# Normalised attention rows copied by a transfer and transposed as float32r with a lag of four slots; token rows transposed as float32r

## The chip, the cores and the metric

The kernel runs on one core of one Trainium2 chip. The metric is the device time of one execution in microseconds (us), lower is better; where several executions are timed, their median counts. All profile rows come from one profiled execution of the same program.

## The reference

Gated causal attention over 8 batches of 8 heads, 576 tokens, head dimension 64, followed by a normalised two-layer feed-forward network on the 4608 tokens of width 512. Everything is float32.

```python
scores = scale * (q @ k.T) + cum[:, None] - cum[None, :]      # cum: cumulative log of the gate f
attn = softmax(where(causal, scores, -1e9))
x = concat_heads(attn @ v)                                     # (8, 576, 512)
xn = (x - mean(x)) / sqrt(var(x) + 1e-6) * g_ln
out = x + relu(xn @ w_ch1) @ w_ch2                             # 512 -> 2048 -> 512
```

## The kernel before

**Slots.** The order of the work is written out by hand. The attention is cut into 256 *slots*, four for each of the 64 heads: slot t (1 to 4) takes 128 rows of queries, and t = 1 also the first 64 rows (called t = 0). `QT` gives each block's first row, its number of rows and the width `w` of keys that it can see: 64, 192, 320, 448, 576. For each slot a string of letters in `ORDERS` says in which order the pieces are recorded on all engines; from slot 70 on this is `"WwAthQFlMSPNgreamLRB"`. The pieces that matter here:

- `Q` multiplies the queries of the slot with the keys (TensorE, tile `s`, lines 368 to 373). `S` (line 396, VectorE) adds the mask into tile `p` and takes the row maximum, `e` (line 407, ScalarE) exponentiates, and `B` (`normalise`, lines 412 to 414) takes the reciprocal on VectorE and multiplies the rows by it on GpSimd. `p` has three buffers; the 64 rows of t = 0 have their own tile of 64 columns (`corner`).
- `t` (`transpose_unit`) transposes the normalised rows of the slot `LAG` = 2 slots back, in pieces of 64 or 128 columns: 3, 3, 4 and 5 transposes for t = 1, 2, 3, 4, so 15 in each head. The rows are the operand that is loaded into the array and the identity is streamed. Both are float32. The result (tiles `tr`, `tr_4b`) goes to `ph` as float32r by ScalarE (`h`, line 476), and from head 12 on the rounding error goes to `pl` by VectorE (`l`, line 481).
- `A` multiplies with the values one slot after t = 2 and t = 4 were transposed (tile `o`, line 511), `F` and `a` bring the sum to `xs`, which is stored to DRAM.
- `P` prepares the next heads: `raw` (keys and queries, 576 KB) is loaded in slot t = 4 for the head after the next and cast to `hi` by ScalarE (line 339) in the next slot; `prep_v` and the load of the next values `vr` stand in slot t = 3.

**Feed-forward.** In each slot from number 35 on, if its operands are planned to be there, `M` does one of 16 steps of the first layer for a *chunk* of 256 tokens (12 matmuls, tile `h`, lines 588 to 590), `r` and `m` split the result into a float32r pair `hh` on ScalarE (line 596) and VectorE (line 601), and `N` does the second layer for the step of the slot before (6 matmuls, tile `acc`, lines 610 to 612). The halves `w2s` of the second layer's weights come from DRAM, three steps ahead (line 703). A chunk's operand `x` is loaded from the stored attention result (`xr`, line 621); `moe.limit` says how many chunks the attention has finished. Near a chunk's end `rows_load` brings its tokens once more (`xw`) and `chunk_rows` transposes them back to rows, eight float32 transposes for each chunk (tile `xp`), for the residual and the statistics. After the last slot the remaining steps run by themselves.

**Queues.** Every transfer is issued by SyncE (SP), in the order in which it is recorded; a transfer that waits holds all those behind it. PSUM has six banks for all of `s`, `tr`, `o`, `h` and `xp`, taken in turn.

The helper through which all transposes go:

```python
    def tr(out_, in_):
        m = in_.shape[0]
        nc.tensor.transpose(out_, in_, ident[:m, :m])
```

Of the kernel before, what the change touches and what calls it, by code (L numbers as in the profile page):

```python
# [8 lines left out]
F32 = mybir.dt.float32  # L9
F32R = mybir.dt.float32r  # L10
# [5 lines left out]
B, H, S, D = 8, 8, 576, 64  # L16
DM, DFF = H * D, 4 * H * D
P = 128
# [10 lines left out]
W2_LOW = 3  # L29
W2_WAIT = 2  # L30
ALL = 2 * NCHUNK * FT + W2_WAIT
LAG = 2
FIRST_MOE = 35
WARM = 36

# [16 lines left out]
ORDERS = [  # L52
    (0, "WwbQsSthAeMrgFmlLNPaRf"),
    (37, "WwbQSstAMhPelgLNFrfmBRa"),
    (70, "WwAthQFlMSPNgreamLRB"),
]


# [1 line left out]
def attn_moe(ctx: ExitStack, tc: tile.TileContext, qk, v, f, g, w1, w2, out):  # L60
# [245 lines left out]
    def load(n):  # L306
        h = Head()
        h.n, h.plain, h.full = n, n < NPLAIN, n < NFULL
        h.normal = {}
        if h.plain:  # L310
            h.kl = work.tile([66, S], F32, tag="kl", bufs=2, name=f"kl{n}")
            if len(xfs) < 2:
                xfs.append(new_xq(f"xf{n}", F32))
            h.xq = xfs[n % 2]
            nc.sync.dma_start(out=h.xq[0:64, :], in_=qk[n][0:64, 0, :])
            nc.sync.dma_start(out=h.kl[0:64, :], in_=qk[n][0:64, 1, :])
            if n > 0:
                nc.sync.dma_start(out=h.kl[64:66, :], in_=cumd[n])
            return h
        h.raw = late.tile([P, 2, S], F32, tag="raw", bufs=2, name=f"raw{n}")  # L320
        nc.sync.dma_start(out=h.raw, in_=qk[n])
        return h
# [95 lines left out]
    def normalise(h, t):  # L418
        h.normal[t] = True
        if t == 1:  # L420
            softmax_b(h, 0)
        softmax_b(h, t)

    def tr(out_, in_):
        m = in_.shape[0]
        nc.tensor.transpose(out_, in_, ident[:m, :m])  # L426

# [1 line left out]

    def transpose_unit(h, t):
        n = f"{h.n}"
        pt = h.p[t][0]
        work_ = []
        if t <= 2:
            if t == 1:
                h.ph1 = work.tile([P, 704], F32 if h.full else F32R, tag="ph1", bufs=1, name=f"ph1_{n}")
                h.pl1 = None if h.full else late.tile([P, 384], F32R, tag="pl1", bufs=1, name=f"pl1_{n}")
            ph = h.ph1  # L440
            pl = ph if h.full else h.pl1
            tp = bank(f"tr{n}_{t}")
            if t == 1:
                tr(tp[0:64, 0:128], h.p[0][0])
                tr(tp[0:64, 64:192], pt[:, 0:64])
                tr(tp[:, 192:320], pt[:, 64:192])
                work_.append((tp[0:64, 0:192], ph[0:64, 0:192], ph[64:128, 0:192]))
                work_.append((tp[:, 192:320], ph[:, 320:448], pl[:, 0:128]))
            else:
                tr(tp[0:64, 0:128], pt[:, 0:64])  # L450
                tr(tp[:, 128:256], pt[:, 64:192])
                tr(tp[:, 256:384], pt[:, 192:320])
                work_.append((tp[0:64, 0:128], ph[0:64, 192:320], ph[64:128, 192:320]))
                work_.append((tp[:, 128:384], ph[:, 448:704], pl[:, 128:384]))
        else:
            if t == 3:
                h.ph2 = work.tile([P, 9 * P], F32 if h.full else F32R, tag="ph2", bufs=1, name=f"ph2_{n}")
                h.pl2 = None if h.full else late.tile([P, 7 * P], F32R, tag="pl2", bufs=1, name=f"pl2_{n}")
            c = 0 if t == 3 else P
            ph = h.ph2[:, : 8 * P].rearrange("p (k c) -> p k c", k=4)[:, :, c : c + P]  # L460
            pl = None if h.full else h.pl2[:, : 6 * P].rearrange("p (k c) -> p k c", k=3)[:, :, c : c + P]
            tp = bank(f"tr{n}_{t}").rearrange("p (k c) -> p k c", k=4)
            tr(tp[0:64, 0, :], pt[:, 0:64])
            for k in range(1, 4):
                tr(tp[:, k, :], pt[:, 64 + P * (k - 1) : 64 + P * k])
            work_.append((tp[0:64, 0, :], ph[0:64, 0, :], ph[64:128, 0, :]))
            work_.append((tp[:, 1:4, :], ph[:, 1:4, :], pl))
            if t == 4:
                tp = bank(f"tr{n}_4b")[:, :P]
                tr(tp, pt[:, 64 + 3 * P : 64 + 4 * P])  # L470
                work_.append((tp, h.ph2[:, 8 * P :], None if h.full else h.pl2[:, 6 * P :]))
        h.parts = work_
# [156 lines left out]
    def chunk_rows(c, i):  # L629

        tp = bank(f"xp{c.n}_{i}")
        for k in range(KT):
            tr(tp[:, P * k : P * k + P], c.xw[:, k, :])
        xt = m2(f"xt{c.n}_{i}", F32)
        nc.scalar.copy(out=xt, in_=tp)
        if i == 0:
            c.sv = work.tile([P, 2, 2], F32, tag="sv", bufs=2, name=f"sv{c.n}")
            c.rs = work.tile([P, 4], F32, tag="rs", bufs=2, name=f"rs{c.n}")
        bs = work.tile([P, 6], F32, tag="bs", bufs=2, name=f"bs{c.n}_{i}")
        nc.vector.bn_stats(bs, xt)  # L640
        nc.vector.bn_aggr(c.sv[:, i, :], bs)
        c.xt.append(xt)
# [110 lines left out]

    slots = [(n, t) for n in range(B * H) for t in (1, 2, 3, 4)]
    nu = len(slots)
    slots += [None] * (LAG + 1)
    hd = {}

    def start_head(n):
# [10 lines left out]
    for u, slot in enumerate(slots):  # L770

        def before(k):
            return slots[u - k] if u >= k else None

        if slot is not None:
            n, t = slot
            h = hd[n]
        av = None
        if before(LAG + 1) is not None and before(LAG + 1)[1] in (2, 4):
            av = hd[before(LAG + 1)[0]]  # L780
        moe.fetch_low(ALL if wp.done() else wp.ready())
        want = moe.can(wp.ready()) and u >= FIRST_MOE

        def piece(c):
            tu = before(LAG)
            if c == "t" and tu is not None:
                transpose_unit(hd[tu[0]], tu[1])
            elif c == "h" and tu is not None:
                transposed_hi(hd[tu[0]], tu[1])
            elif c == "l" and tu is not None:  # L790
                transposed_lo(hd[tu[0]])
            elif c == "Q" and slot is not None:
                if t == 1:
                    qk_mm(h, 0)
                qk_mm(h, t)
            elif c == "A" and av is not None:
                av_unit(av, before(LAG + 1)[1])
            elif c == "S" and slot is not None:
                if t == 1:
                    softmax_a(h, 0)  # L800
                softmax_a(h, t)
            elif c == "e" and slot is not None:
                if t == 1:
                    softmax_e(h, 0)
                softmax_e(h, t)
            elif c in FILL:
                wp.fill(FILL[c])
            elif c == "s":
                wp.sums()
            elif c == "F" and av is not None:  # L810
                finish(av)
            elif c == "a" and av is not None:
                finish_add(av)
            elif c == "r" and want:
                moe.first_high()
            elif c == "R":
                moe.limit = min(NCHUNK, max(0, u - LAG - 1) // (4 * H) * S // C)
                moe.rest()
            elif c == "L":
                run_later(RSTD)  # L820
            elif c == "M" and want:
                moe.first()
            elif c == "B" and slot is not None:
                normalise(h, t)
            elif c == "b" and before(1) is not None:
                b_n, b_t = before(1)
                if not hd[b_n].normal.get(b_t):
                    normalise(hd[b_n], b_t)
            elif c == "m" and want:
                moe.first_low()  # L830
            elif c == "W":
                due = 1 + min(u, W_CHANGE) / W_SLOTS + max(0, u - W_CHANGE) * W_TICKS
                while not wp.done() and wp.tick_no <= due:
                    wp.tick()
            elif c == "N":
                moe.second()
            elif c == "P":
                prep()

        def prep():  # L840

            if slot is not None:
                if t == 1 and n + 1 < NPLAIN:
                    start_head(n + 1)
                if NPLAIN <= n + 1 < B * H:
                    if t == 1:
                        prep_a(hd[n + 1])
                    if t == 2:
                        prep_b(hd[n + 1])
                    if t == 3:  # L850
                        prep_c(hd[n + 1])
                if t == 4 and NPLAIN <= n + 2 < B * H:
                    start_head(n + 2)
                if not h.full and t == LAG + 1:
                    prep_v(h)
                if t == LAG + 1 and n + 1 < B * H:
                    load_v(hd[n + 1])

        for c in [o for first, o in ORDERS if first <= u][-1]:
            piece(c)  # L860
# [48 lines left out]
```

## Time and profile before

| | before |
|---|---|
| median of three runs | 1228.67 us (1228.44 to 1228.71) |
| profiled execution, its own time | 1229.45 us |
| span of the profiled instructions | 1227.4 us |
| TensorE matmuls (PE) busy | 1205.5 us, 98% of the span |
| weight loads (PEld), beside the matmuls | 1075.7 us, 88% |
| VectorE (DVE) / ScalarE (ACT) / GpSimd (POOL) | 62% / 53% / 35% |
| DMA queue q1 | 49.9% of 16 engines, 189.15 MB |
| mean granted TensorE clock | 0.994 |

A matmul's row in the trace has a start and a modelled end, and successive matmuls overlap, so the durations of a group may add up to more than the time it holds TensorE. What a matmul costs in a full stream is the distance from its start to the next start. In a row that joins several instructions ("x4") the second column runs from the first start to the last end.

### The profile page before, as it was taken

Reading aid. Unit: us, or ns where it says so; the run is one execution under the profiler, and the core shown is the slowest. Engines: PE = TensorE matmul, PEld = TensorE weight load, DVE = VectorE, ACT = ScalarE, POOL = GpSimd, SP = SyncE. Lnnn points to the kernel's source line nnn. Section 1 sums busy time; section 2 is a strip of 40 time slices with the busy share of each in tenths; the row PEclk is TensorE's granted clock in tenths of the full one; section 3 lists DMA queues with packets and bytes.
Section 4 is the critical chain, followed back from the end, with each engine's and each line's share of the span. In section 5 each row is a group of like instructions: output and inputs, shape, how many; then the busy total and the mean of one; then the engine's idle time right before and its main releaser. Section 6 shows DMA issues by size and latency. Waiting matters only on the chain.

```text
span 1227.4 us, 25515 instructions
## 1 busy us (share of the span) xinstructions
PE 1205.5 (98%) x8140; PEld 1075.7 (88%) x8140; DVE 762.5 (62%) x2884; ACT 646.3 (53%) x1920; POOL 425.9 (35%) x533
## 2 busy tenths in 40 slices
PE   7998999899999999999999999999999999999998
PEld 5665889889999999999999999999999999999997
DVE  5787647576767676677767676767676764233232
ACT  5888655455655555556555555556555653112111
POOL 3568534333333444343334343334334330000000
PEclk8999999999999999999999999999999999999999
DMA  6888554354545454455454445445454453443532
GB/s 175 249 244 270 175 163 152 104 162 147 164 139 160 143 153 150 155 173 168 151 168 141 145 148 168 156 140 166 140 156 146 153 154 100 143 125 117 148 109 95
DMA packets 138358, 190.78 MB, mean 155 GB/s; under 512 B 31216, under 2 KB 80624, under 8 KB 138224
## 3 DMA queue, kind: packets, MB, share of 16 engines
q1 hardware_dynamic: 138224, 189.15, 49.9%
q8 instruction: 65, 1.06, 0.3%
q14 instruction: 69, 0.57, 0.2%
HBM read 157.46 MB, written 23.36 MB: 147 GB/s over the span
## 4 chain that ended last, share of the span: by engine, by line
PE 90%; DMA 3%; DVE 3%; ACT 2%; issue 1%; SPq 0%; POOL 0%; DVEq 0%; ACTq 0%; POOLq 0%
PE h L588 11%; PE h L589 11%; PE h L590 11%; PE acc L610 10%; PE acc L611 10%; PE acc L612 10%; PE tr L426 7%; PE o L511 6%; PE s L372 3%; PE s L373 3%; PE o L489 3%; DMA raw<-in_qk_dram 2%; PE s L370 2%; PE xp L426 1%; PE pc L190 1%
## 5 line engine op out<-in xcount | busy, mean ns | idle before, releaser
L414 POOL TENSOR_SCALAR p<-p,st 64x64 f32<-64x64 f32 (+4 forms) x320 | 173.2, 544 | 543.4 <-DVE st L413 185.0
L588 PE MATMUL h<-x,w1h 128*128 128x256 f32 x1152 | 330.1, 287 | 3.9 <-DVE st L412 3.1
L589 PE MATMUL h<-x,w1h 128*128 128x256 f32 x1152 | 326.3, 283 | 1.0 <-DVE st L412 0.6
L590 PE MATMUL h<-x,w1l 128*128 128x256 f32 x1152 | 325.2, 282 | 0.0
L596 ACT ACTIVATE hh<-h 128x256 fp32r<-128x256 f32 x288 | 110.4, 383 | 282.9 <-PE h L590 279.0
L601 DVE SCALAR_TENSOR_TENSOR hh<-h,hh 128x256 fp32r<-128x256 f32 x288 | 121.5, 422 | 186.4 <-ACT hh L596 178.6
L610 PE MATMUL acc<-w2h,hh 128*128 128x512 f32 x576 | 228.0, 396 | 0.5 <-ACT hh L596 0.5
L611 PE MATMUL acc<-w2s,hh 128*128 128x512 f32 x576 | 226.6, 393 | 0.0
L588 PEld LDWEIGHTS h<-x,w1h 128*128 128x128 f32 x1152 | 218.4, 190 | 8.8 <-DVE st L412 3.5
L612 PE MATMUL acc<-w2h,hh 128*128 128x512 f32 x576 | 225.9, 392 | 0.0
L589 PEld LDWEIGHTS h<-x,w1h 128*128 128x128 f32 x1152 | 218.6, 190 | 5.0 <-DVE x L573 2.0
L590 PEld LDWEIGHTS h<-x,w1l 128*128 128x128 f32 x1152 | 218.4, 190 | 0.0
L407 ACT ACTIVATE p<-p,st 64x64 f32<-64x64 f32 (+4 forms) x320 | 178.3, 558 | 47.8 <-DVE st L396 43.9
L476 ACT CAST ph<-tr 64x128 fp32r<-64x128 f32 (+4 forms) x416 | 117.8, 332 | 129.0 <-PE tr L426 99.6
L426 PE MATMUL tr<-identr,p 128*128 128x128 f32 (+1 forms) x896 | 140.9, 273 | 6.5 <-POOL p L414 6.3
L396 DVE CUSTOM_DVE_ANT_0 p<-s,mask 64x64 f32<-64x64 f32 (+4 forms) x320 | 130.5, 420 | 11.2 <-PE s L370 4.0
L481 DVE TENSOR_TENSOR ph<-tr,ph 64x192 fp32r<-64x192 f32 x208 | 62.6, 301 | 113.5 <-ACT ph L476 110.5
L612 PEld LDWEIGHTS acc<-w2h,hh 128*128 128x128 f32 x576 | 108.3, 188 | 25.4 <-DVE st L412 0.2
L426 PEld LDWEIGHTS tr<-identr,p 128*128 128x128 f32 (+1 forms) x896 | 100.7, 130 | 30.3 <-POOL p L414 10.5
L610 PEld LDWEIGHTS acc<-w2h,hh 128*128 128x128 f32 x576 | 109.0, 189 | 13.2 <-ACT hh L596 0.7
L611 PEld LDWEIGHTS acc<-w2s,hh 128*128 128x128 f32 x576 | 109.3, 190 | 12.3
L372 PE MATMUL s<-hi 128*64 128x64 f32 x336 | 109.8, 349 | 1.0 <-POOL hi L350 1.0
(82 smaller groups left out, 1782.1 us busy)
## 6 DMA issues: line engine op xcount, KB each, us to landing
w2s<-w2d SPq DMA_DIRECT2D x288, 256.0 KB
raw<-in_qk_dram SPq DMA_DIRECT2D x56, 576.0 KB
wr<-in_w_dram SPq DMA_DIRECT2D x32, 512.0 KB
vr<-in_v_dram SPq DMA_DIRECT2D x64, 160.0 KB
out_dram<-xt SPq DMA_DIRECT2D x36, 256.0 KB
xq<-hi SPq DMA_DIRECT2D x56, 144.0 KB
xa<-xs SPq DMA_DIRECT2D x32, 160.0 KB
w2d<-wl SPq DMA_DIRECT2D x16, 256.0 KB
```

Source lines behind the costliest of these rows:

```text
L372: mm(sp, h.hi[:, 0, q0 : q0 + m], h.hi[:, 1, a:z], start=True, stop=False)
L396: nc.vector.tensor_tensor_reduce(out=pt[:m, a:z], in0=sp, in1=mask[:m, off + a : off + z], scale=-SCALE, scalar=3.0e38 if i == 0 else st[: ...
L407: nc.scalar.activation(pt[:m, :w], pt[:m, :w], AF.Exp, bias=st[:m, i : i + 1], scale=-1.0, accum_out=st[:m, 2:3])
L414: nc.gpsimd.tensor_scalar(out=pt[:m, :w], in0=pt[:m, :w], scalar1=st[:m, 3:4], scalar2=1.0, op0=ALU.mult, op1=ALU.mult)
L426: nc.tensor.transpose(out_, in_, ident[:m, :m])
L588: mm(ph, w1h[:, k, fs], c.x[k][:, 0, :], start=(k == 0), stop=False)
L589: mm(ph, w1h[:, k, fs], c.x[k][:, 1, :], start=False, stop=False)
L590: mm(ph, w1l[:, k, fs], c.x[k][:, 0, :], start=False, stop=(k == KT - 1))
L601: nc.vector.scalar_tensor_tensor(out=h[:, 1, :], in0=ph, scalar=0.0, in1=h[:, 0, :].bitcast(F32), op0=ALU.max, op1=ALU.subtract)
L610: mm(c.acc[i], h[:, 0, ts_], w2h[:, j, :], start=(j == 0), stop=False)
L611: mm(c.acc[i], h[:, 0, ts_], low, start=False, stop=False)
L612: mm(c.acc[i], h[:, 1, ts_], w2h[:, j, :], start=False, stop=(j == FT - 1))
```

## The change

Rows of heads 18 to 63 are no longer transposed from `p`. One slot after the softmax a new piece `D` issues a transfer on SP from `p` to a new tile `pq`, declared float32r (five transfers for each head, the one of t = 0 beside that of t = 1; the tag is one that the preparation of the weights has finished using, nine buffers). The transfer copies the bits. The transposes read `pq`, stream the float32r identity and write the PSUM tile as float32r. They now come four slots after the softmax and the product with the values five slots after it, so `prep_v` and the load of `vr` move to the slot where the head's first transpose stands, and the point at which a chunk may be loaded moves by two slots. The heads before 18 stay as they were. The token rows (`xw`, which transfers wrote) are read as float32r directly, in all 18 chunks.

```diff
-LAG = 2
+LAG, LAG_MOVED = 2, 4
+MOVED = 18
...
-    (70, "WwAthQFlMSPNgreamLRB"),
+    (70, "WwDAthQFlMSPNgreamLRB"),
...
+        h.lag = LAG if n < MOVED else LAG_MOVED
...
+    def move(h, t):
+
+        for t in (0, 1) if t == 1 else (t,):
+            pt, w = h.p[t][0], QT[t][2]
+            pq = wpool.tile([P, S], F32R, tag="wy", bufs=W_FLOAT, name=f"pq{h.n}_{t}")
+            nc.sync.dma_start(out=pq[:, :w].bitcast(F32), in_=pt[:, :w])
+            h.moved[t] = pq
+
+    def rows_of(h, t):
+        return h.moved.get(t, h.p[t][0])
+
     def tr(out_, in_):
         m = in_.shape[0]
-        nc.tensor.transpose(out_, in_, ident[:m, :m])
+        if in_.dtype == F32R:
+            nc.tensor.transpose(out_.bitcast(F32R), in_, identr[:m, :m])
+        else:
+            nc.tensor.transpose(out_, in_, ident[:m, :m])
...
-            tr(tp[:, P * k : P * k + P], c.xw[:, k, :])
+            nc.tensor.transpose(tp[:, P * k : P * k + P].bitcast(F32R), c.xw[:, k, :].bitcast(F32R), identr)
...
-    slots += [None] * (LAG + 1)
+    slots += [None] * (LAG_MOVED + 1)
...
+        def turn(more):
+
+            for lag in (LAG, LAG_MOVED):
+                b = before(lag + more)
+                if b is not None and hd[b[0]].lag == lag:
+                    return b
+            return None
...
-            tu = before(LAG)
+            tu = turn(0)
...
-                moe.limit = min(NCHUNK, max(0, u - LAG - 1) // (4 * H) * S // C)
+                moe.limit = min(NCHUNK, max(0, u - (LAG if u < 4 * MOVED else LAG_MOVED) - 1) // (4 * H) * S // C)
...
+            elif c == "D":
+                if before(1) is not None and hd[before(1)[0]].n >= MOVED:
+                    move(hd[before(1)[0]], before(1)[1])
...
-                if not h.full and t == LAG + 1:
-                    prep_v(h)
-                if t == LAG + 1 and n + 1 < B * H:
-                    load_v(hd[n + 1])
+            first = turn(0)
+            if first is not None and first[1] == 1:
+                m = first[0]
+                if not hd[m].full:
+                    prep_v(hd[m])
+                if m + 1 < B * H:
+                    load_v(hd[m + 1])
```

On SP, around the load of `raw` for head 42 (slot t = 4 of head 40). The rows name tile, number of the head and buffer. Before:

```order
L703 DMA w2s124_9202<-w2d12_139 128x512
L349 DMA xq9_1286<-hi41_9106 64x576
L329 DMA vr41_9250<-in_v_dram 128x320
L558 DMA xb4_163<-xs38_320_8959 128x256
L703 DMA w2s125_9267<-w2d13_140 128x512
L321 DMA raw42_9300<-in_qk_dram 128x1152
L703 DMA w2s126_9325<-w2d14_141 128x512
```

And with the change, whose line numbers are its own:

```order
L719 DMA w2s122_9320<-w2d10_137 128x512
L431 DMA pq40_2_9322<-p40_2_9292 128x320
L351 DMA xq9_1286<-hi41_9233 64x576
L574 DMA xa4_155<-xs38_0_9090 128x320
L637 DMA xr8_2_9379<-xb3_162 128x256
L719 DMA w2s123_9384<-w2d11_138 128x512
L431 DMA pq40_3_9386<-p40_3_9359 128x448
L323 DMA raw42_9424<-in_qk_dram 128x1152
```

Each slot's list now has a copy of the rows of the slot before, right behind `w2s`; in slot t = 4 it stands ahead of `raw`, and `vr` no longer does.

On TensorE, the beginning of slot t = 1 of head 41, from the product with the values to the scores. Before:

```order
L511 MATMUL o40_2_9327<-ph1_40_9214,vv40_9247 128x320
L511 MATMUL o40_2_9327<-ph1_40_9214,vv40_9247 128x256
L511 MATMUL o40_2_9327<-ph1_40_9214,vv40_9247 128x128
L511 MATMUL o40_2_9327<-pl1_40_9215,vv40_9247 64x256
L511 MATMUL o40_2_9327<-pl1_40_9215,vv40_9247 64x128
L426 MATMUL tr40_3_9335<-identr_74,p40_3_9242 64x128
L426 MATMUL tr40_3_9335<-identr_74,p40_3_9242 128x128 x3
L372 MATMUL s41_0_0_9342<-hi41_9106 64x64
```

And with the change:

```order
L527 MATMUL o39_4_9462<-ph2_39_9330,vv39_9237 128x256 x4
L527 MATMUL o39_4_9462<-ph2_39_9330,vv39_9237 128x128
L527 MATMUL o39_4_9462<-pl2_39_9331,vv39_9237 64x256 x3
L527 MATMUL o39_4_9462<-pl2_39_9331,vv39_9237 64x128
L440 MATMUL tr40_1_9474<-identr_74,pq40_0_9264 64x128
L440 MATMUL tr40_1_9474<-identr_74,pq40_1_9266 64x128
L440 MATMUL tr40_1_9474<-identr_74,pq40_1_9266 128x128
L374 MATMUL s41_0_0_9480<-hi41_9233 64x64
```

Slot t = 1 now multiplies for t = 4 of the head before last and transposes t = 1 of the last head, where it multiplied for t = 2 and transposed t = 3; every slot t now transposes its own t of the head before.

On TensorE, the scores of slot t = 4 of head 25 and what follows them, where chunk 3 ends and chunk 4 begins (in `h3_15` and `h4_0` the chunk stands ahead of the step). Before:

```order
L372 MATMUL s25_4_1_5554<-hi25_5111 128x288
L373 MATMUL s25_4_1_5554<-kl25_5112,xq9_1286 128x288
L588 MATMUL h4_0_5559<-x4_0_5394,w1h_124 128x256
...
L610 MATMUL acc3_0_4648<-w2h_126,hh3_15_5527 128x512
```

And with the change:

```order
L374 MATMUL s25_4_1_5588<-hi25_5138 128x288
L375 MATMUL s25_4_1_5588<-kl25_5139,xq9_1286 128x288
L626 MATMUL acc3_0_4660<-w2h_126,hh3_15_5549 128x512
...
L375 MATMUL s26_1_0_5645<-kl26_5405,xq8_1143 128x192
L604 MATMUL h4_0_5653<-x4_0_5556,w1h_124 128x256
```

The first step of chunk 4 comes one slot later. The same happens to chunk 6 and to no other; before, only chunk 2 had such a slot without a first-layer step, and it keeps it.

More of the change, by code (lines that the diff above doesn't have):

```diff
@@ L308, in load @@
         h.n, h.plain, h.full = n, n < NPLAIN, n < NFULL
-        h.normal = {}
+        h.normal, h.moved = {}, {}
+        h.lag = LAG if n < MOVED else LAG_MOVED
         if h.plain:
@@ L422, in normalise @@
         softmax_b(h, t)
+    def move(h, t):
[6 more added lines that the diff above has]
+        return h.moved.get(t, h.p[t][0])
     def tr(out_, in_):
         m = in_.shape[0]
-        nc.tensor.transpose(out_, in_, ident[:m, :m])
+        if in_.dtype == F32R:
+            nc.tensor.transpose(out_.bitcast(F32R), in_, identr[:m, :m])
+        else:
+            nc.tensor.transpose(out_, in_, ident[:m, :m])
     def transpose_unit(h, t):
         n = f"{h.n}"
-        pt = h.p[t][0]
+        pt = rows_of(h, t)
         work_ = []
@@ L443, in transpose_unit @@
             if t == 1:
-                tr(tp[0:64, 0:128], h.p[0][0])
+                tr(tp[0:64, 0:128], rows_of(h, 0)[:, 0:D])
                 tr(tp[0:64, 64:192], pt[:, 0:64])
@@ L777, in attn_moe @@
             h = hd[n]
-        av = None
-        if before(LAG + 1) is not None and before(LAG + 1)[1] in (2, 4):
-            av = hd[before(LAG + 1)[0]]
+        def turn(more):
[4 more added lines that the diff above has]
+            return None
+        av, av_t = None, 0
+        if turn(1) is not None and turn(1)[1] in (2, 4):
+            av, av_t = hd[turn(1)[0]], turn(1)[1]
         moe.fetch_low(ALL if wp.done() else wp.ready())
@@ L796, in piece @@
             elif c == "A" and av is not None:
-                av_unit(av, before(LAG + 1)[1])
+                av_unit(av, av_t)
             elif c == "S" and slot is not None:
```

## The prediction

> **What bounds the kernel now.** I read the page's busy shares and its chain first, then the stretches, because a share over the whole span mixes the start with the rest.
>
> ```profile
> span 1227.4 us, 25515 instructions
> PE 1205.5 (98%) x8140; PEld 1075.7 (88%) x8140; DVE 762.5 (62%) x2884; ACT 646.3 (53%) x1920; POOL 425.9 (35%) x533
> PE 90%; DMA 3%; DVE 3%; ACT 2%; issue 1%; SPq 0%; POOL 0%; DVEq 0%; ACTq 0%; POOLq 0%
> 120.00:275.00 155.00, 150.51 (x1001) 131.81 (x1000) 96.53 (x368) 85.34 (x255) 64.68 (x76) 0.99 0.49 155
> 275.00:1020.00 745.00, 744.59 (x5258) 685.54 (x5257) 517.75 (x2004) 429.22 (x1298) 287.48 (x364) 1.00 0.49 152
> 666.20:682.30 16.10, 16.10 (x116) 14.85 (x114) 9.79 (x38) 8.81 (x27) 6.39 (x9) 1.00 0.42 131
> 1020.00:1227.40 207.40, 203.62 (x1319) 185.12 (x1317) 61.57 (x188) 38.09 (x98) 0.00 (x0) 1.00 0.40 123
> ```
>
> The last four rows give stretch, length, then busy time of PE, PEld, DVE, ACT and POOL, the granted clock and the DMA share. From 275 to 1020 us, where nearly all of the changed heads lie, TensorE is busy 744.6 of 745 us at full clock, while VectorE, the next, has 70%. The short stretch is one head there: 16.1 us, TensorE busy in all of it. What leaves TensorE there comes out of the time, as long as no one else becomes late. So the price of one transpose decides.
>
> **The price of a transpose now.** The stream of one slot boundary, TensorE alone, start and length in us:
>
> ```profile
> 705.50 0.39 PE L612 MATMUL acc<-w2h,hh 128*128 128x512 f32 x1
> 705.73 0.60 PE L426 MATMUL xp<-identr,xw 128*128 128x128 f32 x4
> 706.08 0.57 PE L511 MATMUL o<-ph,vv 128*128 128x320 f32 x3
> 706.49 0.34 PE L511 MATMUL o<-pl,vv 128*64 128x256 f32 x2
> 706.67 0.60 PE L426 MATMUL tr<-identr,p 128*64 128x128 f32 x4
> 707.02 0.27 PE L372 MATMUL s<-hi 128*64 128x64 f32 x1
> 707.85 0.28 PE L588 MATMUL h<-x,w1h 128*128 128x256 f32 x1
> 707.97 0.28 PE L589 MATMUL h<-x,w1h 128*128 128x256 f32 x1
> L426 PE MATMUL tr<-identr,p x896: 270/272/421, 12.7 to 1020.0; 128*128 128x128 f32 x115, 128*64 128x128 f32 x65
> ```
>
> Four transposes last 0.60 us from the first start to the last end, one of them 0.272 (the last row: minimum, median, maximum in ns). So three distances are 0.328 and one is 0.109 us, for loads of 64 and of 128 columns alike (`tr` and `xp`). The type f32 stands in all rows; which operands are float32r, the code says: `o` and `h` are. Two `h` matmuls of 256 streamed columns are 0.12 apart. The two `o` matmuls of 256 and 128 columns from 706.49 take 0.18 until 706.67, so the one of 128 costs 0.06. That is the nearest row to the new operation: float32r, 128 columns, 0.06 against 0.109.
>
> **The load beside it.** A transpose must also load its rows into the array, and that can be the longer half:
>
> ```profile
> L426 PEld LDWEIGHTS tr<-identr,p 128*128 128x128 f32 x576 | 71.3, 141 | 13.2 <-issue 0.8
> L426 PEld LDWEIGHTS tr<-identr,p 128*64 128x64 f32 x320 | 33.0, 111 | 17.2 <-POOL p L414 10.5 <-issue 1.0
> L511 PEld LDWEIGHTS o<-ph,vv 128*128 128x128 f32 x416 | 62.5, 188 | 7.9 <-DVE ph L481 1.6 <-issue 0.3
> L511 PEld LDWEIGHTS o<-pl,vv 128*64 128x64 f32 x312 | 32.6, 135 | 0.0
> 707.16 0.19 PEld L372 LDWEIGHTS s<-hi 128*128 128x128 f32 x1
> 707.27 0.19 PEld L373 LDWEIGHTS s<-kl,xq 66*128 66x128 f32 x1
> 707.39 0.19 PEld L588 LDWEIGHTS h<-x,w1h 128*128 128x128 f32 x1
> ```
>
> For an ordinary matmul 64 more loaded columns cost 188 - 135 = 53 ns, so 128 hold the load path about 106 ns; the last three rows, whose loads of 128 columns follow each other by 0.11 and 0.12 though the `s` between them streams only 192, say the same. In a transpose 64 more cost 141 - 111 = 30 ns, so 128 take 60. If the transposing load keeps that rate in float32r, load and stream both ask for 0.06. I take 0.060; the bounds are 0.057 (a quarter of the 0.23 that the `acc` matmul of 512 columns takes from 705.50 to 705.73) and 0.109 (nothing saved). At 0.057 the sum below would give 43.4 us instead of 40.9. The Trainium skill ("TensorE: Matmul & The Clock Gate", LDWEIGHTS) gives a load as columns over 1.2 GHz, 107 ns for 128 columns, which speaks against this change. The `s` and `o` loads here agree with it, the transposing ones (30 ns for 64 columns) do not; rival 2 says what it would make of the time.
>
> **The sum.** Changed transposes: 46 heads x 15 = 690, and 18 chunks x 8 = 144, in all 834. Saved: 834 x (0.109 - 0.060) = 40.9 us.
>
> What is added on TensorE's own path: two more slots in which no first-layer step is ready (chunks 4 and 6, because the chunk's release comes two slots later). The steps are not lost, they run later; what costs is the wait around the late start. The one such slot of before is chunk 2's:
>
> ```profile
> 263.87 0.29 PE L588 MATMUL h<-x,w1h 128*128 128x256 f32 x1
> 264.81 0.38 PE L589 MATMUL h<-x,w1h 128*128 128x256 f32 x1 [0.65 <-DVE st L412]
> 265.03 0.28 PE L590 MATMUL h<-x,w1l 128*128 128x256 f32 x1
> 265.48 0.39 PE L511 MATMUL o<-ph,vv 128*128 128x320 f32 x1 [0.17 <-DVE ph L481]
> 271.72 0.28 PE L588 MATMUL h<-x,w1h 128*128 128x256 f32 x1
> 272.70 0.50 PE L610 MATMUL acc<-w2h,hh 128*128 128x512 f32 x1 [0.46 <-ACT hh L596]
> ```
>
> Against 0.12 for each `h` matmul the distances are too long by 0.82 (264.81 - 263.87), 0.33 (265.48 - 265.03) and 0.62 (272.70 - 271.72, less three matmuls): 1.8 us. Two more: 3.5 us; between 0 (the loads come in time) and some 7 (each twice as long, since the copies share the queue).
>
> Costed at nothing, with their cover:
> - The 230 copies: 128 partitions x 1640 columns x 4 bytes = 0.84 MB a head, 38.6 MB in all, a fifth of the 189 MB that q1 moves at 49.9%, so some 60% after. Their landing is covered by three slots (a head is 16.1 us long, a slot four) between issue and transpose.
> - `D` waits on SP for GpSimd's product of the slot before, and holds `w2s`, `raw`, `xq`, `kl` and `vr`. `w2s` has three steps in hand. `raw` is the tight one and becomes rival 3.
> - `p` is released by the copy's landing and no longer by the transposes of the slot ahead of its next use; both lie a slot or more ahead.
> - `prep_v` moves from slot t = 3 to t = 1; nothing is added. VectorE's load rises from 70% of 16.1 us to 73% of 15.4 us. The transposes of t = 4 now meet the widest softmax in one slot; TensorE's six banks may wait there for VectorE by tenths of a us. I put 0 to 6 us in the range.
>
> The profiled execution, 1229.45 - 40.9 + 3.5 = 1192.1; the median of the runs stands 0.8 under that execution, so **1191 us**.
>
> **Rivals.**
>
> 1. *The pairs overlap badly.* If half of a streamed transpose (0.053 / 2) adds to the load of the next, one costs 0.06 + 0.025 = 0.085: 834 x 0.024 = 20 us saved, 1212 us. For it: no row shows float32r loads and 128-column streams alternating many times. Against it: the `s` loads above run at their own pace, with the stream beside them. The Trainium skill (same page, Back-to-back issue gap) gives about 81 ns for a sustained stream of such pairs at 128 columns; by that, as an estimate, 834 x 0.028 = 23 us and 1209. No run here shows such a stream yet.
>
> 2. *Little or nothing is saved.* (a) The float32r load goes at the ordinary pace, 106 ns for 128 columns: only the 5 x 46 = 230 loads of 64 columns gain, 230 x 0.049 = 11.3 us, giving 1221. That is also the time by the LDWEIGHTS rule above. (b) A transpose that must carry all 32 bits may stream as long whatever its declared type: 0.109 stays, the late chunks cost 3.5, and the end is 1232, slower. For both: the trace has no float32r transpose at all. Against (b): declared float32r halves the stream in every other group.
>
> 3. *`D` makes `raw` late* (ends slower). How lateness of `raw` reaches TensorE can be seen in before:
>
> ```profile
> 704.09 0.46 SPq L321 DMA_DIRECT2D raw<-in_qk_dram  x1
> 709.41 0.68 ACT L339 CAST hi<-raw 128x576 fp32r<-128x576 f32 x1 [1.03 <-DMA raw<-in_qk_dram]
> 271.56 0.67 ACT L339 CAST hi<-raw 128x576 fp32r<-128x576 f32 x1 [2.80 <-DMA raw<-in_qk_dram]
> 272.26 0.38 ACT L596 ACTIVATE hh<-h 128x256 fp32r<-128x256 f32 x1
> 266.07 0.60 PE L426 MATMUL tr<-identr,p 128*64 128x128 f32 x4
> 702.72 0.64 POOL L414 TENSOR_SCALAR p<-p,st 128x448 f32<-128x448 f32 x1
> 702.05 0.49 PE L426 MATMUL tr<-identr,p 128*64 128x128 f32 x3
> ```
>
> ScalarE waits for `raw`, the `hh` of the slot waits behind that cast, and the second layer of the next slot for `hh` (0.46 us idle at 272.70). There the cast began 271.56 - 266.07 = 5.5 us into slot t = 1 and TensorE lost 0.6, so it may begin about 4.9 in. Usually it begins 709.41 - 706.67 = 2.7 in: 2.2 us of room. With the change, `raw` follows the copy of t = 3, which waits for GpSimd's product; that ended 703.36, 1.3 us into slot t = 4 (702.05). The copy's issue adds some 0.4, so `raw` goes out 1.8 in, where it now goes 704.09 - 702.05 = 2.0 in, since the load of `vr` no longer stands ahead of it. It shares the engines with 0.2 MB of copy. So it should land within the room. It turns the sign if it comes 2.2 + (40.9 - 3.5)/46 = 3.0 us later in every head; at 4 us later the loss is 1.8 x 46 = 83 us against 37 gained: 1274.
>
> **Chances.** The forecast with its own range 1185 (0.057 and no new wait) to 1198 (the 6 us of VectorE): 0.58. Rival 1: 0.14. Rival 2a: 0.06, 2b: 0.10. Rival 3: 0.05. The remaining 0.07: the price is right and smaller waits on VectorE or the banks take back 7 to 30 us (1198 to 1222). The range 1185 to 1222 holds all but 2b, rival 3 and the fringes. A difference of 0.2% (2.5 us) is about what a measurement of this kernel tells from no change. Faster: 0.58 + 0.14 + 0.06 + 0.07 = 0.85. Rival 2b ends 0.3% slower, near that limit, so 0.03 of it goes to no change: 0.03 same, 0.12 slower.
>
> **What would show it.** In the changed profile the `tr` and `xp` groups of four should last about 0.45 us instead of 0.60 (three times 0.06 and one latency of 0.27), and between 300 and 1000 us TensorE should stay busy over 99% with heads of 15.3 us. `pq` appears as 230 issues, with waits of SP for `p` from GpSimd that no one on TensorE inherits. Two new waits of about 2 us stand at the first steps of chunks 4 and 6. ScalarE's wait for `raw` stays near 1 us. I am wrong if a float32r transpose is spaced by over 0.07 us, or if TensorE shows waits in every head: for `hh` (rival 3), or for a bank that VectorE still reads.

## The result and the profile after

The change makes the kernel slower: median 1245.18 us of four runs (1242.34 to 1248.88) against 1228.69 (1228.44 to 1232.29), ratio 1.0129, 95% interval 1.0094 to 1.0164. The forecast was 1191. The profiled execution took 1246.79 us.

The page of the changed kernel, rows that answer to those of before:

```profile
span 1245.0 us, 26040 instructions
PE 1203.7 (97%) x8140; PEld 1069.0 (86%) x8140; DVE 756.8 (61%) x2884; ACT 642.3 (52%) x1920; POOL 426.0 (34%) x533
q1 hardware_dynamic: 171344, 226.85, 59.2%
PE 52%; DMA 5%; DVE 2%; ACT 2%; SPq 1%; issue 1%; DVEq 0%; ACTq 0%; POOLq 0%; POOL 0%
```

Its stretch of the changed heads and, behind it, four stretches of the same execution (length, then busy time of PE, PEld, DVE, ACT and POOL, granted clock, DMA share, GB/s):

```profile
275.00:1020.00 745.00, 723.51 (x5141) 660.94 (x5140) 500.50 (x1979) 417.94 (x1281) 287.25 (x363) 0.99 0.65 200
406.00:409.40 3.40, 3.40 (x11) 2.81 (x12) 2.58 (x12) 2.52 (x10) 2.11 (x3) 0.50 0.26 83
525.50:532.30 6.80, 5.93 (x20) 4.77 (x21) 4.87 (x21) 4.90 (x16) 2.11 (x4) 0.50 0.17 49
546.00:552.80 6.80, 6.44 (x27) 5.99 (x28) 4.07 (x17) 3.19 (x10) 4.04 (x5) 0.50 0.52 163
921.40:924.80 3.40, 3.40 (x18) 3.01 (x17) 2.39 (x8) 2.29 (x7) 2.12 (x3) 0.51 0.71 217
```

TensorE is idle for 21.5 of the 745 us where it had been idle for 0.4, and for 20.4 us it runs at half clock, which costs another 10. Before, its clock was 1.00 in that stretch.

An ordinary head did become shorter. The first score matmul of slot t = 1 in two successive heads, after the change and, in the second fence, before it:

```profile
750.17 0.21 PE L374 MATMUL s<-hi 128*64 128x64 f32 x1
765.81 0.21 PE L374 MATMUL s<-hi 128*64 128x64 f32 x1
```

```profile
674.06 0.28 PE L372 MATMUL s<-hi 128*64 128x64 f32 x1
690.13 0.28 PE L372 MATMUL s<-hi 128*64 128x64 f32 x1
```

15.64 us against 16.07, not the 15.3 that was forecast. And a few heads are far longer. The chain of one of them, head 58's load of `raw`, first on SP:

```profile
902.24 0.58 SPq L637 DMA_DIRECT2D xw<-xb  x1
902.88 0.45 SPq L637 DMA_DIRECT2D xw<-xa  x1
...
906.69 0.43 SPq L637 DMA_DIRECT2D xr<-xb  x1
907.23 0.36 SPq L719 DMA_DIRECT2D w2s<-w2d  x1
907.70 0.47 SPq L431 DMA_DIRECT2D pq<-p  x1
908.58 0.48 SPq L351 DMA_DIRECT2D xq<-hi  x1
909.16 0.52 SPq L574 DMA_DIRECT2D xa<-xs  x1
909.79 1.23 SPq L637 DMA_DIRECT2D xr<-xa  x1
911.07 0.42 SPq L637 DMA_DIRECT2D xr<-xb  x1
911.59 0.38 SPq L719 DMA_DIRECT2D w2s<-w2d  x1
912.06 0.47 SPq L431 DMA_DIRECT2D pq<-p  x1
912.59 0.58 SPq L323 DMA_DIRECT2D raw<-in_qk_dram  x1
```

then on ScalarE and TensorE:

```profile
912.00 0.21 PE L374 MATMUL s<-hi 128*64 128x64 f32 x1
919.45 0.67 ACT L341 CAST hi<-raw 128x576 fp32r<-128x576 f32 x1 [5.37 <-DMA raw<-in_qk_dram]
920.15 0.38 ACT L612 ACTIVATE hh<-h 128x256 fp32r<-128x256 f32 x1
920.59 0.50 PE L626 MATMUL acc<-w2h,hh 128*128 128x512 f32 x1 [3.14 <-ACT hh L612]
```

SP issues one transfer after another, nearly without a pause, from 902 to 913 us: the first of the two loads of a chunk's token rows (`xw`) falls on a border between the stored pieces `xa` and `xb` and takes eight transfers, where four do otherwise. In the median head `raw` goes out 3 us ahead of the first scores of slot t = 1; here it goes 0.6 us behind them (912.59 against 912.00). It lands 6.9 us later, ScalarE's cast begins 7.4 us into the slot, and TensorE waits 3.1 us for `hh`. Just behind that wait, at 921.4, the clock is halved for 3.4 us. The Trainium skill ("TensorE: Matmul & The Clock Gate", The HAM clock gate) says that an idle window of about 3.4 us puts the array to half clock. The lengths of the stretches above, 3.4 or 6.8 us, agree with such a window; the waits ahead of them were shorter. Three are waits for `hh` of 3.1 to 3.2 us. The fourth stretch, at 546.0, comes behind a wait of 2.2 us at the late start of chunk 6, while a wait of 2.1 us for `hh` at 457.8 has none behind it.

For heads 22 to 63 I measured in the traces how far `raw` is issued ahead of that first score matmul, and when its cast begins behind it (median, 90th percentile, longest):

| kernel | issued ahead, us | cast begins, us | heads over 4.9 |
|---|---|---|---|
| before | 3.0 | 2.1, 2.7, 3.7 | 0 |
| changed | 3.0 | 2.5, 5.4, 7.7 | 6 |

The prediction put the limit at 4.9 us, counted from the transposes ahead of those scores, 0.35 us earlier (706.67 against 707.02), so it is about 4.5 in this table. The same six heads pass either limit, and they are the six in which TensorE waits for `hh`, by 0.3 to 3.2 us.

### The profile page after: what moved, and what is told of

Its sections match the earlier page's. It is cut to its first block, busy times and chain, and to the rows that moved or that the text cites. A ratio compares the mean times of both kernels' runs of the same rounds, so it can differ in the third digit from the quotient of the medians.

```text
span 1245.0 us, 26040 instructions
## 1 busy us (share of the span) xinstructions
PE 1203.7 (97%) x8140; PEld 1069.0 (86%) x8140; DVE 756.8 (61%) x2884; ACT 642.3 (52%) x1920; POOL 426.0 (34%) x533
## 3 DMA queue, kind: packets, MB, share of 16 engines
q1 hardware_dynamic: 171344, 226.85, 59.2%
## 4 chain that ended last, share of the span: by engine, by line
PE 52%; DMA 5%; DVE 2%; ACT 2%; SPq 1%; issue 1%; DVEq 0%; ACTq 0%; POOLq 0%; POOL 0%
PE h L605 7%; PE h L604 7%; PE h L606 7%; PE acc L626 7%; PE acc L627 7%; PE acc L628 7%; DMA raw<-in_qk_dram 4%; PE o L527 4%; PE s L374 2%; PE tr L440 2%; PE s L375 2%; ACT p L409 1%; SPq L637 1%; DMA xr<-xb 1%; PE xp L649 0%
## 5 line engine op out<-in xcount | busy, mean ns | idle before, releaser
L626 PE MATMUL acc<-w2h,hh 128*128 128x512 f32 x576 | 229.1, 398 | 12.8 <-ACT hh L612 12.8
L497 DVE TENSOR_TENSOR ph<-tr,ph 64x192 fp32r<-64x192 f32 x208 | 62.6, 301 | 92.1 <-ACT ph L492 65.4
L374 PE MATMUL s<-hi 128*64 128x64 f32 x336 | 106.4, 339 | 0.3 <-DVE st L398 0.3
L375 PE MATMUL s<-kl,xq 66*64 66x64 f32 x336 | 98.6, 298 | 0.7 <-DMA xq<-hi 0.7
L497 DVE TENSOR_TENSOR pl<-tr,ph 128x128 fp32r<-128x128 f32 x208 | 95.2, 458 | 4.6
```

Source lines behind the costliest of these rows:

```text
L374: mm(sp, h.hi[:, 0, q0 : q0 + m], h.hi[:, 1, a:z], start=True, stop=False)
L375: mm(sp, xq, kl, start=False, stop=True)
L497: nc.vector.tensor_tensor(out=lo, in0=tp, in1=hi.bitcast(F32), op=ALU.subtract)
L626: mm(c.acc[i], h[:, 0, ts_], w2h[:, j, :], start=(j == 0), stop=False)
```

## Experiments

All kernels were run beside the kernel before; its medians, 1228.60 to 1230.97, differ from group to group, and each ratio is against its own.

**Token rows alone.** The kernel before with one line changed:

```diff
-            tr(tp[:, P * k : P * k + P], c.xw[:, k, :])
+            nc.tensor.transpose(tp[:, P * k : P * k + P].bitcast(F32R), c.xw[:, k, :].bitcast(F32R), identr)
```

> Only the token rows are transposed as float32r (144 transposes, no copy, lag 2 everywhere). If the price read from the changed kernel's trace holds (about 0.085 us instead of 0.109, since a head's 15 transposes shortened it by 16.06 - 15.64 = 0.42 us or less): 144 x 0.024 = 3.5 us, 1225 us. If the price were the predicted 0.060: 1221.6. If tokens' transposes gained nothing: 1228.7.

Measured 1228.78 us against 1230.01, ratio 0.9983 (0.9972 to 0.9994): 0.7 to 3.4 us gained. A gain, of the size that 0.085 us gives at most; 0.060 is out.

**The price by itself.** Behind the kernel's end six streams, each like this one:

```diff
+    for i in range(96):
+        nc.tensor.transpose(sp[:, P * (i % 4) : P * (i % 4) + P].bitcast(F32R), wide, identr)
```

> The kernel before, and behind its end six streams of 96 each on TensorE alone: transposes from 128 and from 64 loaded columns, as float32 and as float32r, and ordinary float32r matmuls of the same shapes. Prediction's price: float32r 0.060 us for both widths against 0.109. What the changed kernel's heads say: near 0.085 on the mean of ten loads of 128 and five of 64 columns. If the load path sets it: 64 columns near 0.06, 128 columns near 0.09 to 0.11, and the ordinary matmuls of 128 near 0.11.

The streams in its trace (`full` is float32, `round` float32r, `plain` an ordinary float32r matmul), and the loads of three of them by form:

```profile
1223.59 10.64 PE L875 MATMUL full<-identr,w1h 128*128 128x128 f32 x96
1234.07 10.64 PE L878 MATMUL full<-identr,w1h 128*64 128x128 f32 x96
1244.46 8.40 PE L881 MATMUL round<-identr,w1h 128*128 128x128 f32 x96
1252.70 6.00 PE L884 MATMUL round<-identr,w1h 128*64 128x128 f32 x96
1258.54 10.88 PE L887 MATMUL plain<-identr,w1h 128*128 128x128 f32 x96
1269.26 5.92 PE L890 MATMUL plain<-identr,w1h 128*64 128x128 f32 x96
L887 PEld LDWEIGHTS plain<-identr,w1h 128*128 128x128 f32 x96 | 10.8, 192 | 0.0
L875 PEld LDWEIGHTS full<-identr,w1h 128*128 128x128 f32 x83 | 9.1, 141 | 0.0
L881 PEld LDWEIGHTS round<-identr,w1h 128*128 128x128 f32 x96 | 8.3, 141 | 0.0
```

From start to start of the streams: float32 0.109 us for both widths; float32r 8.24/96 = 0.086 with 128 columns loaded and 5.84/96 = 0.061 with 64; an ordinary matmul 0.112 and 0.061. The 128 streamed columns are the same in all of them, so with 128 columns loaded the price hangs on the load; with 64 it is about what the stream alone takes (a quarter of an `acc` matmul's 0.23 is 0.057). The load's own row says 141 ns whether float32 or float32r. The 30 ns by which a row falls with 64 columns fewer are near the 25 by which the price falls (0.086 - 0.061), but loads do not follow each other at 30 ns for 64 columns.

In the heads less is gained than in these streams. One slot's group of three transposes and the `s` behind it, in the run with the lag alone (below, float32) and in the changed kernel:

```profile
692.25 0.49 PE L443 MATMUL tr<-identr,p 128*64 128x128 f32 x3
692.49 0.39 PE L374 MATMUL s<-hi 128*128 128x320 f32 x1
692.73 0.31 PE L375 MATMUL s<-kl,xq 66*128 66x320 f32 x1
```

```profile
689.13 0.37 PE L440 MATMUL tr<-identr,pq 128*64 128x128 f32 x3
689.34 0.38 PE L374 MATMUL s<-hi 128*128 128x320 f32 x1
689.56 0.32 PE L375 MATMUL s<-kl,xq 66*128 66x320 f32 x1
```

The group's row is shorter by 0.12 us, but from its start to that of the second `s` it is 0.43 us against 0.48, so 0.05 saved, where the streams say 0.048 + 2 x 0.023 = 0.09. Both times the first `s` takes longer than the second of the same width (0.22 and 0.24 against some 0.15): part of the transposes' cost stands there. So the prediction's sign, a group of four that lasts 0.45 us, did appear (at 693.03) without the price that it stood for. Why 0.04 us of the gain are missing behind such a group is open.

**The lag without copies.** The rows stay float32 in nine buffers and are transposed from there, four slots later:

```diff
-    (70, "WwDAthQFlMSPNgreamLRB"),
+    (70, "WwAthQFlMSPNgreamLRB"),
...
+            pt = (work.tile([P, S], F32, tag="p", bufs=3, name=f"p{nm}") if h.n < MOVED
+                  else wpool.tile([P, S], F32, tag="wy", bufs=W_FLOAT, name=f"p{nm}"))
```

> The changed kernel without copies: heads 18 to 63 keep their rows in nine float32 buffers and are transposed from them as float32, four slots after the softmax; token rows stay float32r. Against before only the lag and 144 float32r transposes differ. Theory 'hold': no wait for raw; the two late chunks cost what they cost in the run with the copies on ScalarE (some 6 to 8 us of waits and half clock there), less 2 to 3.5 us for the token rows: 1231 to 1237 us. Rival 'lag': the big waits of the changed kernel are here too, above 1250 us.

Measured 1230.15 us against 1228.60, ratio 1.0010 (0.9998 to 1.0023). That is just under what theory 'hold' expected. With some 2 us gained by the token rows the lag costs about 3.5. It has none of the large waits.

**The copies without the rest.** The kernel before; `D` issues the copies, nothing reads them, and `p` is transposed as before:

```diff
+            nc.sync.dma_start(out=pq[:, :w].bitcast(F32), in_=pt[:, :w])
...
-    (70, "WwAthQFlMSPNgreamLRB"),
+    (70, "WwDAthQFlMSPNgreamLRB"),
```

> The kernel before, with the 230 copies of heads 18 to 63 issued on SP at the beginning of each slot, and nothing else: the transposes read p at lag 2 as float32, nothing reads the copies. Theory 'hold': the loss of the change (about 35 us against its faster transposes) is made by these transfers on SP alone, so this kernel is slower than before, 1240 to 1265 us, with TensorE waiting for hh behind a late raw. Rival 'lag' (the late chunks and the new alignment of the slots make the loss): 1229 to 1233 us.

Measured 1272.45 us, ratio 1.0377 (1.0323 to 1.0432): 44 us lost by transfers whose data nobody uses, more than I expected. ScalarE's wait for `raw` before and in this run (us in total, times, longest), and TensorE's two largest waits in it:

```profile
ACT hi L339 <- DMA raw<-in_qk_dram: 42.1, 42, 4.2
ACT hi L340 <- DMA raw<-in_qk_dram: 129.8, 50, 6.1
PE o L519 <- DVE ph L489: 10.9, 18, 1.3
PE acc L618 <- ACT hh L604: 10.0, 13, 2.2
```

So a late `raw` reaches TensorE here by two paths. One is `hh`, as the prediction said. The other it did not have: ScalarE's late cast delays its half of `hh` or of a chunk's operand `x`, VectorE's half waits for that, `ph` stands behind it on VectorE, and the product with the values (`o`) waits for `ph`. The waits that the profile counts on both paths make 21 of the 44 us.

**Wait or bytes.** The same unread transfers, once with the same bytes from a constant tile, so without the wait for GpSimd, and once with the wait but 8 columns only:

```diff
-            nc.sync.dma_start(out=pq[:, :w].bitcast(F32), in_=pt[:, :w])
+            nc.sync.dma_start(out=pq[:, :w].bitcast(F32), in_=w1h[:, 0, :w].bitcast(F32))
```

> The kernel before, with 230 unread transfers on SP of the same sizes and places as the unread copies that cost 44 us, but from the constant tile w1h instead of p: same bytes from SBUF to SBUF, same issues, no wait for GpSimd. Theory 'hold by waiting': nearly all of the 44 us goes, 1228 to 1236 us. Rival 'bytes and issues': 1255 us or more.

```diff
-            nc.sync.dma_start(out=pq[:, :w].bitcast(F32), in_=pt[:, :w])
+            nc.sync.dma_start(out=pq[:, :8].bitcast(F32), in_=pt[:, :8])
```

> The kernel before, with the unread copies cut to the first 8 columns of p: the same 230 issues on SP with the same waits for GpSimd, a fiftieth of the bytes. Theory 'hold by waiting': the loss stays, 1255 to 1275 us. Rival 'bytes': it goes, 1228 to 1236 us. If wait and bytes each hurt only with the other, both this run and the one without waits are well below 1272.

Bytes without the wait: 1269.46 us against 1229.44, ratio 1.0344 (1.0312 to 1.0376). Wait without the bytes: 1243.62, ratio 1.0118 (1.0088 to 1.0148). My theory that SP's wait makes the loss fell: without it 40 of the 44 us stay. The wait alone, with its issues, costs 14. That lies between the two ranges that I gave. No run has the issues alone. Wait and bytes act on the same quantities:

| kernel | issued ahead, us | issue to cast where ScalarE waited, us | cast begins, us |
|---|---|---|---|
| before | 3.0 | 5.1 | 2.1, 2.7, 3.7 |
| wait, no bytes | 1.9 | 4.8 | 3.2, 3.7, 5.4 |
| bytes, no wait | 1.9 | 6.3 | 4.4, 5.7, 7.1 |
| copies, both | 1.3 | 5.7 | 3.9, 5.6, 7.4 |

The 230 issues (0.47 us each on SP in the median) with the wait or with the bytes take 1.1 us of the lead, with both 1.7, and the bytes lengthen the flight by about a us. With the wait alone only one head's cast begins over 4.9 us in, and TensorE waits 0.8 us for `hh` but 3.9 for `ph`: the limit of 4.9 us is that of `hh` alone.

**Is it `raw` alone?** Its load two slots earlier, into a buffer that is free by then; with the unread copies, in the kernel before, and in the changed kernel:

```diff
-                if t == 4 and NPLAIN <= n + 2 < B * H:
+                if t == (2 if n >= 18 else 4) and NPLAIN <= n + 2 < B * H:
```

> The kernel before with the unread copies on SP (which cost 44 us), and raw for heads 20 to 63 recorded in slot t = 2. If the late raw carries nearly all of the loss: 1229 to 1240 us. If the copies' bytes, issues and waits hurt by other transfers as much: above 1252 us.

> The kernel before with raw recorded in slot t = 2 and nothing else. TensorE waited 0.5 us for hh behind raw there, so no change: 1227 to 1230 us. If it gains 5 us or more, the gain of the cured versions is not that of the float32r transposes.

> The changed kernel, with the load of raw for heads 20 to 63 recorded in slot t = 2 instead of t = 4 (its buffer is free by then). Theory 'raw late' (SP issues raw too late, ScalarE's cast of it holds hh, TensorE waits and its clock drops): the waits for hh near 400, 455, 523, 543 and 917 us vanish and the time falls by the 24 us of waits and about 10 us of half clock, to 1208 to 1215 us. Rival 'something else is late too' (xr, xq or w2s take the place of raw): above 1225 us.

With the unread copies: 1230.95 us against 1230.97, ratio 1.0002 (0.9986 to 1.0017). The copies' whole 44 us are gone, with their wait, their issues and their bytes all still there:

```profile
275.00:1020.00 745.00, 743.59 (x5249) 684.76 (x5248) 514.46 (x2003) 431.00 (x1302) 288.71 (x365) 1.00 0.66 203
```

In the row, TensorE is busy 743.6 of 745 us at a DMA share of 0.66; of its waits for `hh` none is left, of those for `ph` 0.2 us. In the kernel before, the earlier `raw` gives 0.9988 (0.9973 to 1.0003), no change that can be told. In the changed kernel it gives 1222.35 us against 1230.01, ratio 0.9927 (0.9907 to 0.9946): 23 us less than the changed kernel (24 when each is taken against its own runs of before), and faster than before. Its trace has no wait for `hh` left. That is short of the 1208 to 1215 that I expected. What is left there, two of TensorE's waits and the two stretches at half clock:

```profile
PE o L527 <- DVE pl L497: 3.0, 2, 1.9
PE o L527 <- DVE ph L497: 1.0, 3, 0.5
528.40:535.20 6.80, 6.51 (x28) 5.90 (x28) 4.21 (x14) 3.10 (x9) 4.05 (x5) 0.50 0.92 281
893.60:897.00 3.40, 3.40 (x16) 3.21 (x16) 2.40 (x11) 2.86 (x10) 0.74 (x1) 0.51 0.72 225
```

The half clock costs 5 us, and starts on TensorE that come too late add 8 (excess distances over 0.35 us, from 275 us on), most of them at the late start of chunk 6 and at two chunk ends, where VectorE has the chunk's statistics beside the widest rows. No run took these away by themselves.

**Copies out of `raw`'s way.** Behind the piece `P` on SP, and on ScalarE's queue behind the exponentials:

```diff
-    (70, "WwDAthQFlMSPNgreamLRB"),
+    (70, "WwAthQFlMSPDNgreamLRB"),
```

> The changed kernel, with the copies recorded behind the piece P, so that raw no longer follows the copy of its slot. If raw is late because this one copy stands ahead of it (its wait for GpSimd and its issue, about 1 us): 1225 to 1235 us. If it is late because SP, held once in each slot, can no longer run ahead and meets the bursts of 8 to 10 transfers near the chunk ends without a reserve: hardly better, 1238 to 1246 us.

```diff
-    (70, "WwDAthQFlMSPNgreamLRB"),
+    (70, "WwAthQFlMSPNgreDamLRB"),
...
-            nc.sync.dma_start(out=pq[:, :w].bitcast(F32), in_=pt[:, :w])
+            nc.scalar.dma_start(out=pq[:, :w].bitcast(F32), in_=pt[:, :w])
```

> The changed kernel with the same copies issued by ScalarE, behind the exponentials of the slot, so that SP's list has none of them. Bytes and landing places are the same. Theory 'hold' (SP's order and its waits make raw late): raw goes out early again, 1208 to 1216 us. Rival 'traffic' (the copies' bytes slow raw down on the DMA engines): raw still lands late, above 1230 us. [...]

Measured 1222.73 us (ratio 0.9940, 0.9922 to 0.9957) and 1220.51 us (0.9930, 0.9914 to 0.9947). Moving the copies behind `P` gives back 22 us, more than either account had expected. `raw` is then issued 4.5 us ahead in the median, and no cast begins over 4.8 us into the slot. The edit moves the copies of all slots, so it does not show that the one ahead of `raw` did it alone. From ScalarE's queue the same bytes do not bring the loss either.

**Both cures, and fewer slots of lag.** Copies on ScalarE or behind `P`, each with the early `raw`; and copies behind `P` with a lag of three:

> Both cures together: copies issued by ScalarE behind the exponentials, and raw for heads 20 to 63 recorded in slot t = 2. ScalarE's remaining waits for raw (29.6 us in the run with the copies on ScalarE) should go. If those waits still cost TensorE something: 1215 to 1219 us. If what remains is the two late chunk starts with their waits and half clock and the load-bound price of the transposes: no better than either cure alone, 1219 to 1223 us.

> Copies on SP, but behind the piece P, and raw recorded in slot t = 2. If SP's burst near the chunk ends still hurts through another transfer (xw, late for the token rows, or xr): 1219 to 1223 us as with either alone. If raw was all that was left: 1214 to 1218 us.

```diff
-LAG, LAG_MOVED = 2, 4
+LAG, LAG_MOVED = 2, 3
```

> The changed kernel with the copies behind the piece P (as in the run that gave 1222.7 us) and a lag of three slots instead of four: one late chunk start instead of two, and another alignment of the slots. If the rest of the loss there is the late chunks with their waits and half clock (3 to 6 us each): 1217 to 1220 us. If it is the traffic or the copies' landing (now a slot less room): 1222 us or more.

Measured 1219.83 (ratio 0.9913, 0.9896 to 0.9931), 1223.34 (0.9943, 0.9922 to 0.9963) and 1236.07 us (1.0058, 1.0033 to 1.0083). With `raw` out of danger once, nothing more comes of doing it twice. A lag of three slots is too short: there TensorE waits for the copies themselves, as it did in no other version:

```profile
PE tr L440 <- DMA pq<-p: 18.1, 15, 2.5
```

**More on ScalarE's queue.** Each copy issued twice there, and the unread copies of the kernel before issued there:

```diff
+            again = wpool.tile([P, 2 * DM], U32, tag="wr", bufs=W_RAW, name=f"again{h.n}_{t}")
+            nc.scalar.dma_start(out=again[:, :w].bitcast(F32), in_=pt[:, :w])
```

> The kernel with the copies on ScalarE, each issued twice, the second time into a buffer that nothing reads: 38.6 MB more. Theory 'hold' (bytes are not what the change loses by): 1220 to 1226 us. Rival 'traffic': the same again as the copies would have cost by their bytes, over 1235 us.

> The kernel before with the unread copies issued by ScalarE instead of SP; nothing else differs from the run in which they cost 44 us. Theory 'hold': most of the 44 us goes, 1228 to 1238 us. Rival 'traffic': they stay, over 1255 us.

Measured 1300.72 us (ratio 1.0564, 1.0542 to 1.0587) and 1244.02 us (1.0113, 1.0088 to 1.0138). The first decides nothing about bytes: TensorE waits there for VectorE (28.0 us for `pl`) and VectorE for ScalarE (133.9 us for `ph`, 65.4 in the changed kernel), whose next instructions stand behind each pair of issues (0.47 and 0.61 us in its rows), and for `raw` it waits less than the changed kernel (26.9 us against 82.7). The second, in neither of its ranges, says that in the kernel before, too, the other queue takes 30 of the 44 us away; the other 14 were not taken apart.

## Why the prediction was wrong

**The price of a transpose was mis-sized.** The prediction took 0.060 us for all 834, since load and stream "both ask for 0.06". Measured alone: 604 with 128 loaded columns at 0.086 and 230 with 64 at 0.061, so 604 x 0.023 + 230 x 0.048 = 25 us and not 40.9. In the heads it is 16.07 - 15.64 = 0.43 us, or 0.35 against the 15.99 us of a head in the run with the lag alone: 46 x 0.35 = 16 us there, where the price in streams would give 46 x 0.47 = 22. The failed step is the reading of 141 - 111 = 30 ns as the rate of the load path, by which 128 columns would take 60. Rival 1 had the price, 0.085. Whether by its mechanism, a part of the stream added to the load, no run tells: nothing of the kind shows in the ordinary stream (0.112 for a load that the prediction read as 0.106), and the transposing load was not timed without its stream. The Trainium skill's 81 ns for such pairs ("TensorE: Matmul & The Clock Gate", Back-to-back issue gap) is near the 0.086 measured; its load rule of 107 ns for 128 columns fits the ordinary stream (0.112) and not the transposing one.

**Rival 3 happened, in a form that was priced wrongly.** It had a chance of 0.05. The mechanism was told right: `raw` late, its cast late, `hh` late, TensorE idle, with a limit of 4.9 us that the changed kernel's trace bears out. Three steps failed. First, "So it should land within the room" was read off one ordinary head. The heads at chunk ends, where SP has up to ten transfers for `xw` and `xr` to issue, were not looked at; there SP had been ahead of the work before, and the copies, their issues and their waits took that lead. In an ordinary head the forecast was right: `raw` goes out 3.0 us ahead, as before. Second, "It shares the engines with 0.2 MB of copy" was left without a price; the unread copies' bytes lengthen the flight by about 1 us. Third, the price was counted as if lateness had to come in every head, and without the clock. Six heads were enough, three of them with waits of 3.1 to 3.2 us and half clock behind each: 12.8 us of waits for `hh` and, for 13.6 us at half clock, 6.8 more make 20 of the 23 us that the early `raw` gives back. The fourth stretch at half clock belongs to the late start of chunk 6 (the second row) and has its like in the run with the early `raw`, at 528.4.

```profile
PE acc L626 <- ACT hh L612: 12.8, 6, 3.2
PE h L604 <- ACT x L588: 3.3, 4, 2.2
```

One factor of the prediction is wrong without consequence: the widths 64 to 576 add up to 1600 columns and not 1640, so the copies are 37.7 MB in all and not 38.6; q1 moves 226.85 - 189.15 = 37.70 MB more.

**What held.** The late chunks and the lag cost about 3.5 us, as forecast, though in part by luck: in the trace of the run with the lag alone about half of the late starts stand at chunk 6, hardly any at chunk 4, and the rest where `o` waits for `ph` (at 452 and 517 us), which was not forecast. TensorE is what bounds an ordinary head, before and after; VectorE's 73% did no harm there. The transposes never wait for their copies at a lag of four.

**The sum as measured**, for the 16.5 us between the medians: transposes -16 in the heads and -2 in the token rows, lag +3.5, late `raw` +23, and 8 more, of which the waits and the half clock at the two late chunk starts and the chunk ends are the candidates. That remainder is a difference of the other rows and was not taken apart by a run.

## What to carry to other kernels

When a transfer is added to a queue that runs ahead of the work, look for the transfer behind it with the least lead, and read its lead and its landing in the worst place of the loop, where the queue has its bursts, not in an ordinary turn. Loading that one earlier cost a single condition here and took away a loss of 44 us to which the added transfers' bytes (40 us with their issues) and their waits (14 with the issues) had contributed. Of the kernels run, the changed one with its copies on ScalarE's queue and the early `raw` has the lowest median (1219.83 us, ratio 0.9913), below the kernel before and the changed one; the copies on ScalarE's queue alone (0.9930) cannot be told from it. And when a price is read from a group of joined rows, check it by the start of what comes behind the group.

## What the hardware showed unexpectedly

A float32r transpose of 128 x 128 takes 0.086 us in a stream where an ordinary float32r matmul of that shape takes 0.112 and the float32 transpose 0.109; with 64 loaded columns both float32r forms take 0.061. A wait of 3.1 us on TensorE cost half as much again, because 3.4 us at half clock came behind it; a wait of 2.2 us was followed by 6.8 us at half clock, one of 2.1 us by none. A transfer takes SP mostly 0.35 to 0.6 us to issue, so ten in a row (902.24 to 907.23) hold everything behind them for 5 us, more than a slot's 4.
